# Split last rows, q transposes of three batches moved to DMA, single head transposes, and two planner constants in a fused attention and dense-layer kernel

## The chip, the cores and the metric

One core of one Trainium2 chip runs the kernel. The metric is device time in microseconds (us), the median of several executions. The kernel before: 322.27 us (320.4 to 323.14). A profile is one execution, and its span (first to last instruction) is about 2 us less than its time.

In the profiles PE is TensorE's matmuls, PEld its weight loads, DVE VectorE, ACT ScalarE, POOL GpSimd, SPq SyncE's sequencer.

## The reference, cut to what matters

```
attn: q, k, v of (batch 8, heads 8, seq 576, dim 64)
  heads 0-3 ("band"):    query i sees keys i-31 .. i
  heads 4-7 ("strided"): query i sees keys j <= i with j % 32 == i % 32
  softmax, times v, heads joined -> x (4608, 512)
dense: h = x @ w_in (512 -> 2048); g = s * relu(h)^2 + b; out = g @ w_out, float32
```

## The kernel before

The kernel is written as small steps. A planner with a clock of its own decides, when the program is built, in which order each engine gets its instructions, from estimated costs and landing times. Each engine then runs its list in order. So a changed estimate changes the program.

```python
class Plan:
    LAT = {"A": 70.0, "V": 70.0, "P": 70.0, "D": 12000.0, "X": 12000.0}   # estimated latencies, ns
    ...
    def flush(self):      # of the posts that are ready, the earliest; on the engine that ends first
        ...
        eng = min(p[1], key=lambda e: max(self.free[e], r) + p[1][e])

def pair_post(b, name, mm, key):     # bring two heads side by side, for one 128-wide transpose
    ...
    plan.post([key], {"A": 810, "V": 350, **({"P": 900.0} if b in (1, 2, 3) else {})}, g, ...)

def trans(name, j, group):
    alone = loc and b < HEAD_T       # HEAD_T = 1: the first batch has no pair copies
    def f():
        if alone:
            for e in range(2):       # two transposes of 64 columns
                nc.tensor.matmul(out=st["p" + name][64 * e:64 * e + 64, ...],
                                 lhsT=loaded[b, name + "l"][:, at:at + D], ..., is_transpose=True)
            return
        nc.tensor.matmul(out=st["p" + name][...], lhsT=src, ..., is_transpose=True)

k_by_dma = b >= (KB_DMA if loc else 3)
q_by_dma = b >= (QB_DMA if loc else QS_DMA)     # QB_DMA = 8 (never), QS_DMA = 4

def rows_before(b, mm, key):         # copies rows inside v_loc once v's load has landed
    plan.post([key], {"P": 800.0} if b == 0 else {"A": 700.0, "V": 350.0}, g, ...)

def landing(cost):                   # estimate of when a load lands
    ring = max(ring, plan.t + 2000.0) + cost
    return ring + (6000.0 if plan.t > 60000.0 else 0.0)

def second(eng):                     # second batch (index 1), issued from GpSimd's queue
    weights_out(range(1))            # first quarter of w_out
    fetch_qk(1)
    weights_out(range(1, 4))
    load_vl(1)
    ...
# ... cut ...
```

GpSimd issues most of the loads, and computes a little; SyncE issues output stores and DMA transposes. Each is one list in order.

The softmax here doesn't subtract the row's maximum and nothing guards it: scores larger than these inputs give would overflow.

## Time and profile before

| | before |
|---|---|
| median time | 322.27 us |
| span of the profile | 319.6 us |
| TensorE busy | 311.2 us, 97% |
| TensorE without a matmul, 7.5 to 36 us | 2.93 us |
| the same, 60 to 210 us | 0.54 us |
| start of the last eviction | 315.77 us |
| from there to the end | 3.84 us |

Rows four and five are the stretch's length less PE's busy time in the stretch table that the prediction shows (28.50 - 25.57 and 150.00 - 149.46). Spans are printed to 0.1 us; for the time from the last eviction to the end I use the trace's own span (319.61 here). Two groups that the change shortens (after the bar: busy us, mean ns of one, then idle time before):

```profile
L388 PE MATMUL ps_t<-ident,qp 96*128 96x96 f16 x78 | 5.8, 206 | 1.1 <-DVE qp L294 1.1
L388 PE MATMUL ps_t<-ident,qs 72*128 72x72 f16 x48 | 2.9, 197 | 0.0
```

The 206 ns is the length of one matmul in the trace, up to its modelled end. These overlap, so what one costs is the distance between starts: 43 ns for the first group, 33 ns for the second.

### The profile page before, as it was taken

To read this page: it belongs to the slowest core of one execution; us is meant where nothing else is said; L and a number is where in the kernel's file an instruction comes from. 1 tells how busy PE (TensorE), PEld (TensorE's weight loads), DVE (VectorE), ACT (ScalarE), POOL (GpSimd) and SP (SyncE) were. 2 spreads that over 40 slices of the span, in tenths; PEclk is the share of its full clock that TensorE was granted. 3 is DMA by queue.
4 is the path that set the end of the run, shared out by engine and by line. 5 is a ranking of instruction groups with operands and counts; after the bars stand their busy time and mean duration, and the time that the engine had idled before them with its cause. 6 is when DMAs were issued, how large, how long until landed. Compare 5 with 4: busy or idle time off the path is not lost.

```text
span 319.6 us, 6136 instructions
## 1 busy us (share of the span) xinstructions
PE 311.2 (97%) x2268; PEld 175.2 (55%) x2268; DVE 197.9 (62%) x545; ACT 162.8 (51%) x309; POOL 92.0 (29%) x134
## 2 busy tenths in 40 slices
PE   8898999999999999999999999999999999999995
PEld 3764555666556556555546655655544544444442
DVE  5565888889777887778558677865433324333211
ACT  1875962689737675756408836830541533333100
POOL 7552568800870189056207510000000000000000
PEclk9999999999999999999999999999999999999999
DMA  7999999994999799979999999222200000100021
GB/s 125 188 211 205 214 169 156 229 134 42 92 147 162 99 77 165 163 105 176 159 191 159 165 103 169 69 72 103 72 33 33 33 35 33 66 36 33 35 96 66
DMA packets 91527, 36.89 MB, mean 115 GB/s; under 512 B 73898, under 2 KB 85290, under 8 KB 91498
## 3 DMA queue, kind: packets, MB, share of 16 engines
q0 software_dynamic: 53264, 18.08, 57.0%
q1 hardware_dynamic: 38234, 18.43, 29.4%
q8 instruction: 17, 0.28, 0.4%
q14 instruction: 12, 0.10, 0.1%
HBM read 36.84 MB, written 10.62 MB: 148 GB/s over the span
## 4 chain that ended last, share of the span: by engine, by line
PE 87%; DMA 8%; POOL 1%; DVE 1%; ACT 1%; issue 0%; SPq 0%; POOLq 0%; DVEq 0%
PE ps_f L698 39%; PE ps_f L663 36%; PE ps_s L505 4%; DMA kl<-in_k_dram 4%; PE ps_a L557 4%; PE ps_t L388 2%; DMA w_out_sb<-in_v_dram 2%; DMA ql<-in_q_dram 2%; PE ps_a L721 1%; PE ps_t L605 1%; POOL v_loc L294 1%; PE ps_f L557 0%; ACT qD_loc L294 0%; DVE gT L687 0%; PE ps_f L388 0%
## 5 line engine op out<-in xcount | busy, mean ns | idle before, releaser
L663 PE MATMUL ps_f<-xT,w_in_sb 128*128 128x512 f16 x568 | 148.0, 379 | 0.0
L698 PE MATMUL ps_f<-w_out_sb,gT 128*128 128x512 f16 x576 | 146.6, 379 | 0.4 <-DVE gT L687 0.4
L681 ACT ACTIVATE u<-ps_f 128x512 f16<-128x512 f32 x137 | 81.2, 597 | 87.4 <-PE ps_f L663 74.4
L687 DVE TENSOR_TENSOR gT<-u 128x512 f16<-128x512 f16 x144 | 59.5, 418 | 55.5 <-ACT u L681 54.9
L663 PEld LDWEIGHTS <-w_in_sb 128*128 128x128 f16 x576 | 61.8, 114 | 43.7
L698 PEld LDWEIGHTS <-gT 128*128 128x128 f16 x576 | 53.8, 98 | 53.6 <-DVE gT L687 0.8
L519 ACT ACTIVATE pt<-ps_s 128x384 f16<-128x384 f32 (+2 forms) x92 | 42.1, 489 | 10.4 <-PE ps_s L505 9.7
L709 DVE SCALAR_TENSOR_TENSOR o<-ps_f,s_sb,bcs 128x512 f32<-128x512 f32 x36 | 26.9, 747 | 21.9 <-PE ps_f L698 21.4
L557 PEld LDWEIGHTS <-pt 72*72 72x72 f16 (+1 forms) x448 | 31.3, 119 | 15.1 <-issue 0.2
L583 DVE TENSOR_TENSOR x_nat<-ps_a,rec 72x256 f16<-72x256 f32 (+1 forms) x76 | 35.0, 461 | 1.6
L572 DVE RECIPROCAL rec<-ps_a 72x4 f32<-72x4 f32 (+1 forms) x76 | 13.7, 180 | 20.1 <-PE ps_a L557 20.0
L272 POOL DMA_DIRECT2D v_loc<-in_v_dram x28 | 21.0, 759 | 6.0 <-PE ps_s L505 2.1
L294 ACT COPY qD_loc<-ps_t 64x576 f16<-64x576 f16 x22 | 13.9, 631 | 8.4 <-PE ps_t L388 8.1
L527 DVE TENSOR_TENSOR pt<-pt,mask_loc 128x384 f16<-128x384 f16 x42 | 14.4, 360 | 2.0 <-ACT pt L519 1.7
L557 PE MATMUL ps_a<-v_str,pt 72*72 72x65 f16 x204 | 15.3, 197 | 0.0
L277 POOL DMA_DIRECT2D v_str<-in_v_dram x16 | 13.0, 814 | 6.6 <-PE ps_a L557 3.0
L527 DVE TENSOR_TENSOR pt<-pt,mask_str 72x432 f16<-72x432 f16 (+1 forms) x42 | 14.0, 344 | 1.3 <-ACT pt L519 1.1
L753 POOL COPY gate<-kT 1x1 f16<-1x1 f16 x6 | 1.4, 230 | 40.3 <-DMA kT<-ks 40.3
L249 POOL DMA_DIRECT2D kl<-in_k_dram x16 | 11.8, 756 | 0.0
L557 PE MATMUL ps_a<-v_loc,pt 128*96 128x65 f16 x150 | 11.7, 206 | 0.0
L505 PE MATMUL ps_s<-qD_loc,kT_loc 128*128 128x192 f16 x68 | 10.5, 246 | 0.1
L905 PE MATMUL ps_f<-ones 128*128 128x512 f16 (+2 forms) x30 | 9.0, 432 | 1.4 <-DVE ones L227 1.1
(108 smaller groups left out, 241.5 us busy)
## 6 DMA issues: line engine op xcount, KB each, us to landing
out_dram<-o SPq DMA_DIRECT2D x36, 256.0 KB, 4.8
ql<-in_q_dram POOLq DMA_DIRECT2D x8, 288.0 KB, 6.4
w_out_sb<-in_moe_w_out_dram POOLq DMA_DIRECT2D x4, 512.0 KB, 11.3
v_loc<-in_v_dram POOLq DMA_DIRECT2D x28, 72.0 KB, 8.3
qs<-in_q_dram POOLq DMA_DIRECT2D x6, 288.0 KB, 7.7
ks<-in_k_dram POOLq DMA_DIRECT2D x6, 288.0 KB, 7.8
kl<-in_k_dram POOLq DMA_DIRECT2D x4, 288.0 KB, 8.4
kl<-in_k_dram POOLq DMA_DIRECT2D x16, 72.0 KB, 4.4
```

The lines of the kernel that those rows point to most:

```text
L272: nc.gpsimd.dma_start(out=vl[LPAD:128, h, :, 0:D], in_=v_band(b, h))
L294: {"A": nc.scalar.copy, "V": nc.vector.tensor_copy, "P": nc.gpsimd.tensor_copy}[eng](**kw)
L505: nc.tensor.matmul(out=st["s", g][0:nk, c:c + 2 * nq], lhsT=(st["k"][:, i * nq:i * nq + nk] if loc else st["k"][:, i, 0:SQ]), rhs=st["q"][ ...
L519: nc.scalar.activation(out=pt[0:nk, 0:2 * n].rearrange("k t c -> k (t c)"), in_=st["s", g][0:nk, 0:2 * n * nq], func=AF.Exp, scale=scale)
L527: nc.vector.tensor_tensor(out=pt[0:nk, 0:2 * n], in0=pt[0:nk, 0:2 * n], in1=mask, op=ALU.mult)
L557: nc.tensor.matmul(out=st["a"][0:nq, j % per, :], lhsT=st["pt", g][0:nk, i, :], rhs=vt[0:nk, 2 * mm + e, j, :])
L583: nc.vector.tensor_tensor(out=st["x"][:, j0:j0 + per, 64 * e:64 * e + 64], in0=st["pa", e, j][0:nq, 0:per, 0:D], in1=st["rec", e, j][0:nq, ...
L663: nc.tensor.matmul(out=gts["h", T, ft], lhsT=w_in_sb[min(ft // 4, 2)][:, ct].rearrange("p (c x l) -> p c l x", x=128, l=4)[:, max(ft // 4 ...
L681: nc.scalar.activation(out=gts["u", T, ft], in_=gts["h", T, ft], func=AF.Relu)
L687: nc.vector.tensor_tensor(out=gts[T][:, ft, :], in0=u, in1=u, op=ALU.mult)
L698: nc.tensor.matmul(out=gts["o", T, ts], lhsT=gts[T][:, ft, ts * 128:(ts + 1) * 128], rhs=w_out_sb[:, ft, :], start=(ft == 0), stop=(ft == ...
L709: nc.vector.scalar_tensor_tensor(out=o, in0=gts["o", T, ts], scalar=s_sb[:, 0:1], in1=bcs, op0=ALU.mult, op1=ALU.add)
```

## The change

Its intent: shorten the uncovered end; take transposes off TensorE; spare the second batch the pair copies; and change two of the planner's landing estimates.

```diff
-    LAT = {..., "D": 12000.0, "X": 12000.0}
+    LAT = {..., "D": 12000.0, "X": 7000.0, "Y": 12000.0}
-    KB_DMA, QS_DMA, XS_DMA = 4, 4, 4
-    QB_DMA = B
+    QB_DMA, KB_DMA, QS_DMA, XS_DMA = 6, 4, 3, 4
-    HEAD_T = 1
+    HEAD_T = 2
-  loaded[b, "qT2"] = inp.tile([...], FP16, tag="kp", name="qT2")
+  loaded[b, "qT2"] = inp.tile([...], FP16, tag="vs" if b < KB_DMA else "kp", name="qT2")
-            plan.post([("xd", id_)], {"X": 1300.0}, x_in, [("xT", b, m)])
+            plan.post([("xd", id_)], {"Y": 1300.0}, x_in, [("xT", b, m)])
-    def ff2(T, ts, ft, group):
+    def ff2(T, ts, ft, group, part=0, parts=1):
+        n = DM // parts
+        cols = slice(part * n, part * n + n)
         ...
-                rhs=w_out_sb[:, ft, :], ...)
+                rhs=w_out_sb[:, ft, cols], ...)
-            s.posts = [([key, ("bcs",)], {"V": 750}, ev, [group])]
+            s.posts = [([id_, ("bcs",)], {"V": 750 / parts + 60}, ev, [group])]
-        return ring + (6000.0 if plan.t > 60000.0 else 0.0)
+        return ring + (6000.0 if plan.t > 60000.0 else 600.0)
         for ts in range(4):
+            parts = 2 if T == NBLK - 1 and ts == 3 else 1
+            for part in range(parts): ...
```

## The prediction

> **What bounds the kernel now.** I read the page's busy shares first, then TensorE's clock, TensorE's own waits, busy time by stretch, and last TensorE's timeline around the gaps and the end of the run.
>
> The busy shares, and from the slices the granted clock:
>
> ```profile
> span 319.6 us, 6136 instructions
> PE 311.2 (97%) x2268; PEld 175.2 (55%) x2268; DVE 197.9 (62%) x545; ACT 162.8 (51%) x309; POOL 92.0 (29%) x134
> ...
> PEclk9999999999999999999999999999999999999999
> ```
>
> TensorE is busy 97% of the span at full clock. A busy PE need not be a PE at its peak, so I look at its pace: in the stretch from 297.44 us (below) 84 matmuls of 512 columns take 18.29 us up to the end of the last one, about 0.216 us each. The two dense layers have 2 x 576 of them and the bias sum 16: 1168 x 0.216 = 252 us. The rest is attention on TensorE, dummy matmuls at the start, gaps, and the end. The waits of TensorE's matmuls, whole list:
>
> ```profile
> PE ps_f L905 <- DVE ones L227: 1.1, 1, 1.1
> PE ps_t L388 <- DVE qp L294: 1.1, 1, 1.1
> PE ps_t L388 <- ACT qD_loc L294: 0.5, 1, 0.5
> PE ps_a L380 <- ACT qD_loc L294: 0.5, 1, 0.5
> PE ps_f L698 <- DVE gT L687: 0.4, 1, 0.4
> PE ps_f L905 <- DVE x_nat L583: 0.4, 1, 0.4
> PE ps_s L505 <- DVE kTs L294: 0.3, 1, 0.3
> ```
>
> The reader is to see that all seven together are 4.3 us, and that only two of them (1.1 and 0.5, line 388: the transposes of the second batch's pairs) are near what the change touches. By stretch (columns: length, then busy time of PE, PEld, DVE, ACT, POOL, clock, DMA):
>
> ```profile
> 7.50:36.00 28.50, 25.57 (x319) 17.68 (x318) 18.34 (x52) 20.39 (x44) 14.00 (x23) 1.00 1.19 203
> 36.00:60.00 24.00, 24.00 (x223) 14.53 (x223) 20.58 (x58) 13.00 (x26) 16.85 (x22) 1.00 1.40 180
> 60.00:210.00 150.00, 149.46 (x1197) 88.97 (x1195) 115.62 (x338) 97.65 (x189) 55.37 (x78) 1.00 1.25 135
> 210.00:300.00 90.00, 90.00 (x445) 44.73 (x444) 35.00 (x80) 30.45 (x51) 0.00 (x0) 1.00 0.14 45
> ```
>
> After 36 us TensorE lacks about half a microsecond in all. So VectorE, ScalarE and the DMA queues, which are busier there than elsewhere, hardly hold it up, and time comes off in three places only: TensorE instructions that vanish, gaps before 36 us, and the tail after the last matmul. The gap at 30 us, on TensorE's timeline (start, length, instruction, idle before):
>
> ```profile
> 28.83 1.03 PE L663 MATMUL ps_f<-xT,w_in_sb 128*128 128x512 f16 x4
> 30.91 0.43 PE L388 MATMUL ps_t<-ident,qp 96*128 96x96 f16 x6 [1.05 <-DVE qp L294]
> 31.18 0.60 PE L663 MATMUL ps_f<-xT,w_in_sb 128*128 128x512 f16 x2
> ...
> 34.08 0.41 PE L388 MATMUL ps_t<-ident,kp 96*128 96x96 f16 x6 [0.54 <-ACT qD_loc L294]
> ```
>
> And the tail, all engines:
>
> ```profile
> 297.44 18.29 PE L698 MATMUL ps_f<-w_out_sb,gT 128*128 128x512 f16 x84
> ...
> 315.77 0.75 DVE L709 SCALAR_TENSOR_TENSOR o<-ps_f,s_sb,bcs 128x512 f32<-128x512 f32 x1 [2.70 <-PE ps_f L698]
> 316.55 0.33 SPq L713 DMA_DIRECT2D out_dram<-o  x1
> ```
>
> TensorE ends at 315.73, the eviction at 316.52, and the output transfer with its completion fills the rest to 319.6: 3.9 us that nothing covers.
>
> **What the Trainium skill says.** "TensorE: Matmul & The Clock Gate", section "Back-to-back issue gap", gives N/2.4 + 2.5 ns for a warm matmul of N columns, so 216 ns at 512 and 109 at 256: two halves cost no more than one whole (218 against 216). The trace agrees at 512 (0.216); 256 has not run here, but 192-column score matmuls follow each other every 0.08 us, which the formula gives too and which shows that a weight load hides behind fewer than 256 columns. The same section also claims about 131 ns sustained at 512 columns; this trace denies it. "VectorE: DVE Perf Modes", the cycle table in the section on the TRN2 errata, gives (120 + elements)/0.96 ns for an operation that reads PSUM: 658 ns for the eviction's 512 elements, where the trace has 747. [...]3.1 us pass from the end of the eviction to the end of the span for a 256 KB transfer whose packets occupy only some 0.8 us (317.4 to 318.2).
>
> **The change part by part.**
>
> (1) Last 128 rows in two halves of 256 columns. TensorE: 16 matmuls become 32 half ones, +0.03 us. The last eviction handles half: fixed part and slope from the trace's 747 ns at one element a cycle (512/0.96 = 533, rest 214): 214 + 267 = 0.48, saving 0.27 us. The last transfer has 128 KB in as many packets of half the size; its 0.8 us of packets shrinks, but the packets' fixed cost stays, so I count 0.2 to 0.4, not the full half. The first half leaves 1.7 us earlier and is out of the way. Tail: -0.55.
>
> (2) Band q of the last two batches by DMA. In the instruction order 24 transposes of 96 columns vanish. On the timeline six of them occupy 30.91 to 31.18, 0.27 us: 24/6 x 0.27 = -1.08 us. It adds small casting loads (four per batch for one), four DMA transposes, and spreads by VectorE and ScalarE in place of PSUM copies; these lie beside a saturated TensorE.
>
> (3) Strided q of batch 4 by DMA. 16 transposes vanish; eight occupy 0.26 us (35.46 to 35.72): -0.52 us. Two of the spreads that replace the PSUM evictions land on GpSimd, which was busy 29%.
>
> (4) Band heads of the second batch transposed singly. The pair copies of q and k (VectorE 0.35, ScalarE 0.83 us each) go; 24 paired transposes become 48 single ones. In the first batch 12 single ones took 7.51 to 7.79, 0.28 us, against 0.27 for six pairs: two half-width ones overlap. Cost 4 x 0.01, at most +0.2 if some do not overlap. But the gap does not go with the copy: the copy started at 30.50, which is when q lands, and took only 0.35. In the new order these transposes come after 22 dense matmuls in place of 24, so TensorE reaches them 0.43 us earlier and waits for the same landing, until about 30.55: that gap stays near 1.2 us, and only the two moved matmuls and the shorter start gain. The second gap (0.54) came from ScalarE having done a k pair copy before the q evictions, and should shrink or go. Net -0.4.
>
> (5) The scheduling constants (landing estimates +0.6 us, write-then-transpose estimate 7 us for 12) only reorder. Around 83 and 87 us TensorE now starts about 0.25 and 0.6 us late behind a crowded VectorE and ScalarE; less copying may recover part. -0.2, with either sign possible.
>
> Sum: -0.55 + 0.03 - 1.08 - 0.52 + 0.1 - 0.4 - 0.2 = -2.6 us. 322.27 - 2.6 = 319.7 us, 0.8% less.
>
> **The rivals.** First, the q landing simply takes the copy's place, and the reordering opens new gaps of one or two microseconds elsewhere: for it, the order changes from the second batch on and DMA transposes stand in SyncE's in-order queue with the output stores; against it, TensorE has lost only 0.5 us after 36 us even with that queue. It would give 321 to 322. Second, VectorE and ScalarE relief packs TensorE better: for it, VectorE is busy 86% from 36 to 60 us; against it, TensorE is without a gap there. At most another 1.5 us, 318. Third, GpSimd or the DMA queues become the bound through the extra loads and the in-order spread, delaying later batches: against it, the last 110 us are dense work with TensorE full and almost no loads, so late batches have slack. It would give 323 or more.
>
> **Range and chances.** The kernel before spread over 320.4 to 323.14 in three runs, as much as the gain, so the range must hold both that and the rivals: 317.8 to 321.8. Faster by 2% needs under 315.8, 6.4 us, more than all gaps plus removed work that I can name: 0.03. Slower by 2% needs a stall of 9 us: 0.02. Within 2%: 0.95.
>
> **What would show it.** Right: PE busy some 1.5 us lower with the same shape; the last eviction near 0.48 us and about 3.4 us from the last matmul to the end; single transposes starting right after q lands near 30.5 with a gap of over 1 us; 256-column matmuls 0.11 us apart. Wrong: the gap at 30 us gone (then more gain), new PE waits on a q transposed by DMA or on evictions between 60 and 210 us, or half matmuls slower than 0.11 us.

## The result, and the profile after

The changed kernel takes 318.68 us (317.78 to 319.07, five runs). The ratio to the kernel before is 0.9886, 95% interval 0.9847 to 0.9925. The gain is clear of noise and under 2%. The prediction was 319.7 in 317.8 to 321.8.

The page, and TensorE's waits (total us, times, longest):

```profile
span 315.9 us, 6151 instructions
PE 310.1 (98%) x2268; PEld 175.2 (55%) x2268; DVE 194.5 (62%) x543; ACT 160.8 (51%) x304; POOL 97.1 (31%) x140
```

```profile
PE ps_f L913 <- DVE ones L226: 1.1, 1, 1.1
PE ps_a L379 <- ACT qD_loc L293: 0.5, 1, 0.5
PE ps_f L913 <- DVE x_nat L583: 0.4, 1, 0.4
PE ps_s L505 <- DVE kTs L293: 0.3, 1, 0.3
```

Of the seven waits of before, the ones for the pair copy (1.1), for the bank that ScalarE freed late (0.5) and for a dense layer's input (0.4) are gone. The table by stretch (length, then busy PE) says the same:

```profile
7.50:36.00 28.50, 27.14 (x368) 18.83 (x366) 18.47 (x51) 21.61 (x48) 14.55 (x24) 1.00 1.19 209
60.00:210.00 150.00, 149.99 (x1137) 87.39 (x1136) 112.39 (x331) 93.62 (x180) 58.46 (x83) 1.00 1.27 139
```

Idle falls from 2.93 to 1.36 us in the first and from 0.54 to 0.01 in the second. TensorE's timeline at the former gap:

```profile
26.83 2.75 PE L663 MATMUL ps_f<-xT,w_in_sb 128*128 128x512 f16 x12
29.52 0.45 PE L379 MATMUL ps_f<-ident,ql 96*64 96x96 f16 x12
29.80 0.42 PE L379 MATMUL ps_t<-ident,ql 96*64 96x96 f16 x12
...
31.72 0.45 PE L379 MATMUL ps_f<-ident,kl 96*64 96x96 f16 x12
32.09 0.62 PE L663 MATMUL ps_f<-xT,w_in_sb 128*128 128x512 f16 x2
```

There is no gap before the q transposes, where I had predicted one of over 1 us: in this trace q has landed at 29.19 (before: 30.48), though the change touches nothing that comes before this landing. The experiments come back to that. The end:

```profile
310.79 0.48 DVE L714 SCALAR_TENSOR_TENSOR o<-ps_f,s_sb,bcs 128x256 f32<-128x256 f32 x1 [1.00 <-PE ps_f L703]
...
312.53 0.48 DVE L714 SCALAR_TENSOR_TENSOR o<-ps_f,s_sb,bcs 128x256 f32<-128x256 f32 x1 [1.26 <-PE ps_f L703]
```

The last eviction takes 0.48 us as predicted and is followed by 315.88 - 312.53 = 3.35 us (from its start) instead of 3.84.

### The profile page after: what moved, and what is told of

It is laid out like the page before. It is cut to its first block, busy times and chain, and to the rows that moved or that the text cites. A ratio compares the mean times of both kernels' runs of the same rounds, so it can differ in the third digit from the quotient of the medians.

```text
span 315.9 us, 6151 instructions
## 1 busy us (share of the span) xinstructions
PE 310.1 (98%) x2268; PEld 175.2 (55%) x2268; DVE 194.5 (62%) x543; ACT 160.8 (51%) x304; POOL 97.1 (31%) x140
## 4 chain that ended last, share of the span: by engine, by line
PE 89%; DMA 8%; POOL 1%; issue 0%; SPq 0%; DVE 0%; POOLq 0%
PE ps_f L703 39%; PE ps_f L663 37%; PE ps_s L505 5%; DMA kl<-in_k_dram 4%; PE ps_a L557 4%; DMA w_out_sb<-in_v_dram 2%; DMA ql<-in_q_dram 2%; PE ps_t L387 1%; PE ps_a L726 1%; PE ps_t L605 1%; POOL v_loc L293 1%; PE ps_f L557 0%; SPq L797 0%; POOL ql L251 0%; PE ps_f L387 0%
## 5 line engine op out<-in xcount | busy, mean ns | idle before, releaser
L663 PE MATMUL ps_f<-xT,w_in_sb 128*128 128x512 f16 x568 | 145.7, 379 | 0.0
L703 PE MATMUL ps_f<-w_out_sb,gT 128*128 128x512 f16 (+1 forms) x592 | 144.8, 373 | 0.0
L681 ACT ACTIVATE u<-ps_f 128x512 f16<-128x512 f32 x140 | 82.8, 597 | 98.3 <-PE ps_f L663 85.0
L703 PEld LDWEIGHTS <-gT 128*128 128x128 f16 x592 | 55.6, 98 | 52.5 <-DVE gT L687 0.6
L714 DVE SCALAR_TENSOR_TENSOR o<-ps_f,s_sb,bcs 128x512 f32<-128x512 f32 (+1 forms) x37 | 27.0, 730 | 25.1 <-PE ps_f L703 24.5
L293 ACT COPY xT<-ps_t 128x576 f16<-128x576 f16 x7 | 4.5, 638 | 10.9 <-PE ps_t L605 10.9
```

The source lines that it names most:

```text
L663: nc.tensor.matmul(out=gts["h", T, ft], lhsT=w_in_sb[min(ft // 4, 2)][:, ct].rearrange("p (c x l) -> p c l x", x=128, l=4)[:, max(ft // 4 ...
L681: nc.scalar.activation(out=gts["u", T, ft], in_=gts["h", T, ft], func=AF.Relu)
L703: nc.tensor.matmul(out=gts[id_], lhsT=gts[T][:, ft, ts * 128:(ts + 1) * 128], rhs=w_out_sb[:, ft, cols], start=(ft == 0), stop=(ft == NFT ...
L714: nc.vector.scalar_tensor_tensor(out=o[:, 0:n], in0=gts[id_], scalar=s_sb[:, 0:1], in1=bcs[:, cols], op0=ALU.mult, op1=ALU.add)
```

## The experiments

Twelve runs were made (one of them the changed kernel again), in four jobs with a chip each (the first two on the same one) and the kernel before beside them. Kernels of different jobs are compared by their ratios to it. All gave correct results. The theory was that of the prediction: parts that add up, with time coming off only where TensorE's own list gets shorter. The rivals: the parts work through one another by way of the order; or the larger gain comes from the early q landing.

### One part at a time

**The halves alone.** Edit: `ff2` and its loop as in the diff, all else as before.

> The kernel before with the last 128 rows in two column halves and nothing else. If the tail saving is what the changed kernel's trace shows (3.87 us from the last matmul to the end before, 3.39 after), the end comes 0.5 us after the last matmul sooner: 321.8 against 322.3, and the last eviction takes 0.48 us. Rival (halves cost TensorE as much as they save): 32 half matmuls take over 3.7 us instead of 3.5 and the time stays at 322.3. The scheduler's eviction estimate (810 for 750) also reorders a little from 45 us on; if TensorE's waits between 36 and 210 us change by more than 0.5 us that is the reorder, not the tail.

Measured: 321.43 us, ratio 0.9996 (0.9973 to 1.0019). No gain shows in time, yet the tail is shorter:

```profile
316.96 0.48 DVE L714 SCALAR_TENSOR_TENSOR o<-ps_f,s_sb,bcs 128x256 f32<-128x256 f32 x1 [1.26 <-PE ps_f L703]
```

The span ends at 320.14, 3.19 us after this start, but TensorE's list ended 1.2 us later than before. With the eviction estimate of 810 for 750, TensorE's order differs from before's from 55 us on, and its idle time from 60 to 210 us is 0.89 us in this trace against 0.54. The reshuffled order is thus the likely eater of the tail's gain, and the mean span of all fast runs (319.5 against 319.3) fits; halves with the old estimate, which would show it, did not run.

**Single band heads alone.**

```diff
-    HEAD_T = 1
+    HEAD_T = 2
```

> The kernel before with the second batch's band heads transposed singly and nothing else. My theory: TensorE waits for the landing of the second batch's q, not for its pair copy. Without the later landing estimate this order puts the q transposes after 19 dense matmuls (24 before, 22 in the whole change), so TensorE reaches them about 28.8 us and waits until q lands: a gap near 1.5 us if q lands at 30.5 as in the kernel before, near 0.5 if at 29.2 as in the changed one; the wait of 0.5 us at 34 us goes. Time 321.5 to 322.3 (0 to -0.8 us). Rival (the copy itself was the cost): no gap over 0.5 us whenever q lands, and -1.5 us or more, 320.8 or less.

Measured: 324.65 us, ratio 1.0093 (1.0066 to 1.0119): slower, by about 3 us, which neither theory had. The profile fell in a slow run, so I use of it only which instruction TensorE waits for:

```profile
30.35 0.45 PE L380 MATMUL ps_f<-ident,ql 96*64 96x96 f16 x12 [1.40 <-DMA ql<-in_q_dram]
```

The releaser is now the load itself, which is the prediction's claim: the copy was not the cause of the gap. The copy's own part is what passes from q's landing to the first transpose: 0.43 us before (30.48 to 30.91), 0.04 here (30.31 to 30.35). Where the fast runs lose their 3 us is not shown, as none was profiled; this slow trace has further waits of TensorE after 100 us (2.3, 0.9 and 0.6), the longest of the kind shown next.

**Band q of the last two batches alone.** Edit: `QB_DMA` 6 for 8.

> The kernel before with band q of the last two batches by DMA and nothing else. Theory of removed TensorE work: 24 transposes of 43 ns less, -1.0 us, no new TensorE wait: 321.2. Rival (the DMA queues or GpSimd delay the late batches, or SyncE's queue holds the output stores): TensorE waits appear between 150 and 210 us and the time stays at 322 or rises.

Measured: 320.92 us, ratio 0.9983 (0.9963 to 1.0003). The start of the last eviction, 315.77 before, is here

```profile
314.67 0.75 DVE L708 SCALAR_TENSOR_TENSOR o<-ps_f,s_sb,bcs 128x512 f32<-128x512 f32 x1 [2.70 <-PE ps_f L697]
```

1.10 us sooner, with no new TensorE wait after 36 us: 24 transposes at 0.045 us, as predicted (1.08). This profile's end, from there to 319.19, is 4.52 us, the longest of all traces and 0.7 over before's (the other five with whole last rows have 3.72 to 3.84). In time the gain reads as 0.5 with an interval that just includes 1.1, and none as well.

**Strided q of batch 4 alone.** Edit: `QS_DMA` 3 for 4, and the tile's tag.

> The kernel before with strided q of batch 4 by DMA (and its tile in another pool) and nothing else. Theory of removed TensorE work: 16 transposes of 33 ns less, -0.5 us, and perhaps the late matmul at 87 us (0.6 us) gone with the relief of VectorE and ScalarE: -0.5 to -1.1, 321.2 to 321.8. Rival: the spreads on GpSimd, in its in-order queue, hold later loads back; TensorE waits appear after 90 us and the time does not fall.

Measured: 320.94 us, ratio 0.9965 (0.9944 to 0.9986), 1.1 us less and so within what was expected. Its runs go from 319.67 to 323.46, and the profile caught the longest. TensorE, and then VectorE at that time:

```profile
195.60 0.29 PE L557 MATMUL ps_a<-v_str,pt 72*72 72x65 f16 x4 [2.23 <-DVE x_nat L583]
195.73 2.15 PE L663 MATMUL ps_f<-xT,w_in_sb 128*128 128x512 f16 x6
```

```profile
191.36 0.33 DVE L293 COPY v_loc<-v_loc 32x640 f16<-32x640 f16 x1 [0.27 <-DMA v_loc<-in_v_dram]
194.22 0.32 DVE L293 COPY v_loc<-v_loc 32x640 f16<-32x640 f16 x1 [2.53 <-DMA v_loc<-in_v_dram]
194.58 0.43 DVE L687 TENSOR_TENSOR gT<-u 128x512 f16<-128x512 f16 x1
```

Read from below: VectorE's list has a small copy that needs the last batch's v, and v lands late. VectorE stands 2.53 us, then frees TensorE's bank at 195.5, and TensorE has stood 2.23 us. After that six matmuls take 2.15 us where at full clock they take six times 0.216 plus 0.16, 1.46: from 196.4 to 199.8 us the granted clock is 0.50. One late load, which a busy engine waited for in its list, reached the bound engine and its clock. The expectation's rival, GpSimd issuing v late, is not what happened: its last v load was issued at 178.6 us (before: 179.0) and landed at 194.1 (before: 191.2, with the copy only at 192.6). Why it took 3 us longer is open.

### The constants

**The two constants alone.** Edit: the `LAT`, `x_in` and `landing` lines of the diff.

> The kernel before with the two scheduling constants of the change alone (landing estimates 0.6 us later before 60 us, 7 us for 12 between a write of x and its transposing read). No instruction is added or removed. Theory A (the parts are separate and the constants only reorder): 0 to -0.5 us, 320.8 to 321.3, q transposes still behind a gap of about 1 us at 30 us if q lands at 30.4. Theory B (the constants are what lets the other parts pay, because the write-then-transpose estimate keeps SyncE's queue and so the last batches' loads early): alone still near zero, but a trace without a VectorE wait for v_loc after 180 us.

Measured: 341.54 us, ratio 1.0611 (1.0581 to 1.0641). Both theories fall. TensorE's longest wait, and GpSimd's timeline at its end:

```profile
PE ps_t L388 <- POOL kp L294: 19.5, 1, 19.5
```

```profile
49.69 0.77 POOL L267 DMA_DIRECT2D vs<-in_v_dram  x1
50.50 0.82 POOL L294 COPY kp<-kl 96x768 f16<-96x768 f16 x1
51.27 0.67 POOL L252 DMA_DIRECT2D ql<-in_q_dram  x1
```

With landings estimated 0.6 us later, the planner judged GpSimd the earliest engine for one of the second batch's k pair copies, a copy of 0.8 us. (The run changes both constants. Building the kernel before with one at a time, without a run, puts this copy on GpSimd with the landing constant and leaves it where it was with the other.) In GpSimd's list it stands behind fifteen issues of later loads and a memset, and the issues themselves wait for earlier transfers. Nine of the fifteen belong to later fetches, which the planner books on GpSimd at no time (`{"P": 0.0}` in the kernel). k landed near 31 us, and the copy ran at 50.50.

**The change without single heads.** Edit: `HEAD_T` back to 1.

> The changed kernel with the second batch's band heads transposed as pairs again. Theory: the heads are worth the wait of TensorE for the pair copies, 0.4 us by my prediction and up to 1.5 by the changed kernel's trace, in which both gaps (30 and 34 us) are gone: 319.1 to 320.2 where the changed kernel has 318.7. Rival (the order is what counts, and the heads alone cost 3 us in the first job through a late load): no difference, or a VectorE wait for v_loc after 180 us.

Measured: 340.18 us, ratio 1.0563 (1.0535 to 1.0592), and again one TensorE wait of 19.0 us for that copy on GpSimd. So in the change as it stands, the single heads are what makes the new landing constant bearable: without pair copies there is nothing for GpSimd to be given.

**The change in pairs, GpSimd barred.**

```diff
-    HEAD_T = 2
+    HEAD_T = 1
-    {"A": 810, "V": 350, **({"P": 900.0} if b in (1, 2, 3) else {})}
+    {"A": 810, "V": 350, **({"P": 900.0} if b in (2, 3) else {})}
```

> The changed kernel with the second batch's band heads in pairs again, and GpSimd barred from that batch's pair copies. In the two kernels with the new constants and pairs, a k pair copy stood on GpSimd and TensorE waited 19 to 19.5 us for it. If that queue was the whole cost, the 19 us go, and what is left against the changed kernel is what the copies themselves cost: 0.3 to 1.0 us, 318.6 to 319.3 (the changed kernel in the same job as a yardstick: ratio 0.989 to the kernel before). Rival (pairs with the new constants are bad in themselves): over 322.

Measured: 318.19 us, ratio 0.9901 (0.9883 to 0.992), where the changed kernel has 0.9886 and 0.9890. The 19 us are gone, and with them any measurable use of the single heads: the two kernels cannot be told apart, though intervals of this width would hide the 0.3 us predicted. VectorE copied q at 29.54, as soon as it had landed. TensorE's wait is 0.6 us:

```profile
PE ps_t L387 <- DVE qp L293: 0.6, 1, 0.6
```

**The change without the constants.** Edit: those lines back.

> The changed kernel with the two scheduling constants as before. If the constants carry the head (22 dense matmuls ahead of the q transposes against 19 with the old estimate), TensorE waits for q from about 28.7 us until it lands, a gap of 0.5 (early landing, 29.2) to 1.7 us (late, 30.4), and the time is 0.5 to 1.5 us over the changed kernel: 319.2 to 320.2. If they also carry the late part, a wait of TensorE of about 2 us near 190 to 200 us behind VectorE's v_loc copies comes on top and the time is 321 or more. If they carry nothing: 318.7.

Measured: 319.53 us, ratio 0.9935 (0.9909 to 0.9961) against 0.9890 for the changed kernel in the same job: the constants are worth 0.45%, 1.4 us, once nothing stands on GpSimd. Which of the two is worth it no run separates. In this trace q is early too, and the waits for loads are back (0.4 for q, 0.6 for strided q); idle time from 7.5 to 36 us is 2.48 us (28.50 - 26.02) against 1.36. No late wait appeared near 190 us.

**Heads and constants, without the other three parts.** Edit: the kernel before with `HEAD_T` 2 and the constants.

> The kernel before with the single heads and the new constants, but whole last rows and no further q by DMA. If these two together make the base and the other three parts add what their TensorE work says (1.0 and 0.5 us) and the tail 0.5, this stands 2.0 us over the changed kernel: 320.2 to 320.7, ratio 0.995 to 0.997. If the base already brings the gain that I missed (3.5 measured, 2.6 predicted), ratio about 0.992. If the order it gives has a late load (a wait of over 1 us after 100 us), at or over the kernel before.

Measured: 323.11 us, ratio 1.0053 (1.0026 to 1.0081). Slower than before, although the same head order is part of a kernel that is 1.1% faster. Its profile (its slowest run, 324.83) has TensorE waits of 1.2 and 1.5 us for q of the first two batches and 1.0 us for a mask at 65 us. How much of this the median run has is not known, so what makes this combination slow stays open. It does refute a sum of parts: heads with constants +0.5%, and the missing three parts would have to bring 1.6%, 5 us, of which TensorE's list and the tail explain about 2.

### The landing of q

**The changed kernel again, unaltered.**

> The changed kernel again, unaltered, to see whether its early q landing (29.2 us against 30.3 to 30.8 in four of five traces with other orders, 29.4 in the fifth) is its own or chance. If its own: q lands at 29.2 again, no gap at 30 us, 318.7. If chance: some profile has it at 30.4, a TensorE wait of about 1 us before the q transposes, and a time near 319.5; the ratio to the kernel before is then 0.989 to 0.993.

Measured: 318.27 us (317.82 to 319.03), ratio 0.9890 (0.9862 to 0.9918). The profile fell on the longest of its runs, as the first one had fallen on the shortest of its own. The same instructions in the same order, and yet:

```profile
30.34 0.45 PE L379 MATMUL ps_f<-ident,ql 96*64 96x96 f16 x12 [0.88 <-DMA ql<-in_q_dram]
```

Here is the gap of the prediction, released by the load. What differs is how fast the DMA engines ran between 12 and 16 us (last column: GB/s); first the trace with q early, then this one:

```profile
12.00:16.00 4.00, 3.71 (x73) 3.54 (x72) 2.99 (x10) 3.38 (x9) 2.18 (x5) 1.00 1.26 215
```

```profile
12.00:16.00 4.00, 3.60 (x74) 3.31 (x70) 3.46 (x11) 3.20 (x8) 2.50 (x5) 1.00 1.16 169
```

The stretch is busy with loads that stand ahead of q's; 46 GB/s less for 4 us is 184 KB, 0.9 us at 209 GB/s, an estimate beside the 1.1 us between the two landings (29.19 and 30.30). All thirteen traces with this order of loads divide in the same way: in six, before among them, the stretch has 138 to 178 GB/s and q lands at 30.30 to 31.92; in seven it has 199 to 220 and q lands at 29.16 to 29.73. TensorE's order is the same in all of them up to 28.6 us. So early and late landing are two outcomes of one program, chance as far as these runs show; why the rate differs is open. The honest pair of traces is before against this one, both late. This one's last eviction:

```profile
313.74 0.48 DVE L714 SCALAR_TENSOR_TENSOR o<-ps_f,s_sb,bcs 128x256 f32<-128x256 f32 x1 [1.26 <-PE ps_f L703]
```

| | before | changed, q late | changed, q early |
|---|---|---|---|
| q transposes start | 30.91 | 30.34 | 29.52 |
| TensorE idle, 7.5 to 36 us | 2.93 | 2.49 | 1.36 |
| TensorE idle, 60 to 210 us | 0.54 | 0.21 | 0.01 |
| last eviction starts | 315.77 | 313.74 | 312.53 |
| from there to the end | 3.84 | 3.39 | 3.35 |
| span | 319.6 | 317.1 | 315.9 |

**q and k of the second batch loaded first.**

```diff
-        weights_out(range(1))
         fetch_qk(1)
-        weights_out(range(1, 4))
+        weights_out(range(4))
```

> The changed kernel with the second batch's q and k loads issued ahead of the first quarter of w_out. If what TensorE waits for at 30 us is the landing of q, q lands near 27 us, ahead of need, and neither early nor late landing shows: no wait of over 0.3 us between 25 and 36 us, and 0.3 to 1.0 us under the changed kernel, ratio 0.986 to 0.988. Rival (the wait moves to w_out or to the dense layer's own input weights, which land at 25 to 26.6): a wait of TensorE for w_out near 36 to 40 us or of the first dense matmuls, and no gain.

Measured: 319.29 us, ratio 0.9938 (0.9918 to 0.9959). The gap is gone as expected: the q transposes start right behind dense matmuls, and no wait from there to 36 us is listed for TensorE.

```profile
27.50 0.45 PE L379 MATMUL ps_t<-ident,ql 96*64 96x96 f16 x12
```

The time is nevertheless longer than the changed kernel's, by 1 us or 0.5% (of other jobs; the intervals touch), and no wait for w_out took its place. Its last eviction starts at 313.89, as late as in the changed kernel's trace with q late (313.74). Idle time from 7.5 to 36 us is 1.77 us here, between the two traces above; from 60 to 210 us it is 0.23. One wait removed by another load order did not shorten the run; where the microsecond went is open.

### A candidate

**384 and 128 columns.** The order of all other instructions is the changed kernel's.

```diff
-            parts = 2 if T == NBLK - 1 and ts == 3 else 1
+            parts = (384, 128) if T == NBLK - 1 and ts == 3 else (DM,)
```

> The changed kernel with the last rows split 384 and 128 columns in place of 256 and 256; the order of every other instruction is the same, so nothing else can move. From the last matmul to the end took 3.18 to 3.45 us in the seven traces with halves and 3.77 to 4.57 in the six with whole rows. If the eviction follows 214 ns plus one element a cycle, the last eviction takes 0.35 us (0.48 at halves) and the transfer shrinks a little: 3.1 to 3.3 us, 0.2 us under the changed kernel, which time alone cannot show (ratio 0.988 to 0.990 for both). Rival: 128-column matmuls are held up by their weight loads (over 0.08 us each where 0.056 is the column count's), 16 x 0.03 = 0.4 us lost, and nothing is gained.

Measured: 318.09 us, ratio 0.9893 (0.9862 to 0.9923). The trace:

```profile
311.44 0.62 DVE L714 SCALAR_TENSOR_TENSOR o<-ps_f,s_sb,bcs 128x384 f32<-128x384 f32 x1 [1.85 <-PE ps_f L703]
...
312.33 0.35 DVE L714 SCALAR_TENSOR_TENSOR o<-ps_f,s_sb,bcs 128x128 f32<-128x128 f32 x1 [0.28 <-PE ps_f L703]
```

315.44 - 312.33 = 3.11 us from the last eviction's start, 0.25 less than the changed kernel's 3.35; the eviction is at the expected 0.35, and the 128-column matmuls follow each other every 0.056 us in the trace, so the rival falls. In time it cannot be told from the changed kernel (its median is 0.2 and 0.6 us under that kernel's two, which are of other jobs), and it takes 1.1% less than the kernel before. (Counted from the modelled end of the last matmul, halves gave 3.22 to 3.43 us in seven traces and whole rows 3.76 to 4.56 in six, a little off the limits that the expectation names; here it is 3.15.)

## Why the prediction was right or wrong

It was right in time, range and class, and one step in it was not (5); the measured gain is larger than the predicted 2.6 us: 3.6 by the medians, 3.5 by the second job (mean of the kernel before 321.82, of the changed one 318.35).

- **What bounds the kernel: right.** Every gain and loss found went through TensorE's list, its waits or the tail. PE's busy time fell by 1.1 us (311.2 to 310.1) where the prediction gave 1.5 as a sign; the longer single heads of (4), 0.36 us, make up most of the difference.
- **(1) Tail, -0.55: right within 0.1 us.** Traces: 3.84 to 3.35 and 3.39, -0.45 to -0.49, with the eviction at 0.48 us. Half matmuls came at 0.109 us each.
- **(2) Band q, -1.08: right.** The trace of that part alone: -1.10.
- **(3) Strided q, -0.52: consistent, not shown.** Alone 0.35% or 1.1 us, interval 0.4 to 1.8; it is 16 transposes at 33 ns in the list.
- **(4) Single heads, -0.4: right in mechanism, the cost too low.** The gap is the load's and not the copy's: shown by TensorE's wait for q's load itself, with single heads alone and in the changed kernel's second trace. Barring GpSimd instead gives the same time within 0.3%, so the part itself is worth nothing that shows. The singles cost more than the 0.1 of the sum and its limit of 0.2: in the changed kernel the four groups take 0.28, 0.35, 0.38 and 0.38 us (1.39) where the pairs took 1.03. The prediction read 0.28 from the first group of the first batch; the other three in the same trace take 0.35, 0.38 and 0.38. The 0.28 is that of a group with another group of singles behind it; those with a full-width matmul behind them take longer.
- **(5) Constants, "only reorder ... -0.2, with either sign possible": this is the step that failed.** Beside the other parts they measure -1.4 us, seven times the estimate. Without single heads they cost 20 us, by the wait behind GpSimd's queue, a path that the prediction does not have. I read their effect on the order of the finished kernel and booked most of it under the heads; I did not ask what each would do without the other.

For the matched traces, one execution of each, the sum closes. From before to the changed kernel with q late the last eviction moves by -2.03 us: -1.10 band q (as measured alone), -0.52 strided q (as estimated), +0.36 singles, -0.44 and -0.33 idle time in the two stretches, -2.03 together; the prediction had -2.07 without the tail. With the tail the span falls by 2.5, predicted 2.6.

The medians give about 1 us more. The mean span of the second job's fast runs falls by 3.07 (319.45 to 316.38); the remaining 0.4 of the 3.5 lies outside the span, where the kernel before has 2.4 us and the changed one 2.0. Of the 3.07, the matched pair explains 2.5. Early and late landing differ by 1.2 us in span for one program, so a different share of early landings is enough to fill the rest, but two profiles of the changed kernel (and the early one of the 384 split, whose order is the same up to the last rows) and one of the kernel before do not show those shares. That stays open.

The first rival, q's landing in place of the copy, is what happened in the second profile; its time of 321 to 322 did not, since no new gaps opened. That such gaps do open is shown by the halves alone, the heads alone, strided q alone and heads with constants; the whole change happens to have none. That was luck: no term of the sum covered it.

## What to carry to other kernels

Where a planner fixes each engine's order from estimates, parts of a change do not add up: measure the whole, and take the sum from one pair of traces, part by part, rather than from the times of single-part kernels. Before crediting a removed copy, look at what ends the wait when the copy is gone, and compare traces whose loads landed alike. Do not let a planner put urgent work into a queue that also issues loads, unless it books the issues and their waits too: one 0.8 us copy there cost 19.5 us.

## What the Trainium skill lacked or had wrong

- "TensorE: Matmul & The Clock Gate", section "Back-to-back issue gap": it gives about 131 ns at 512 columns and about 81 ns at 128 for sustained streams of weight loads and matmuls, and calls its formula the isolated case. In this kernel's sustained streams, each matmul with its own weight load, the formula holds: 216 ns at 512, 109 at 256, 56 at 128.
- The same page, section "What's actually happening", has the clock halve after an idle window of about 3.4 us. In the trace of strided q alone, a wait of 2.23 us was enough: 0.8 us after it ended the granted clock was 0.50, for 3.4 us. TensorE had been busy for 1.18 of the 3.41 us before that.
- "VectorE: DVE Perf Modes", section on the TRN2 errata: its table's fixed part of 120 cycles for a PSUM source is too small for this scalar-tensor-tensor operation with fp32 operands, one from PSUM and one from SBUF. 744, 484 and 351 ns at 512, 256 and 128 elements are one element a cycle at 0.96 GHz with a fixed part of 202 to 209 cycles.
- Pages describe the packing of narrow matmuls, but none that I found gives the cost of transposes of 64 columns in pairs: twelve took 0.28 to 0.38 us here, against 0.25 to 0.27 for six of 128.
